# DeltaNet and soft mixture of experts on one core: full 32-column inversions on GpSimd, keys multiplied apart from queries, 24 stores and a re-planned order

## The chip, the cores and the metric

The kernel runs on one core of a Trainium2 chip. A core has a matrix engine (TensorE; PE in the profile, its weight loads PEld) and three others: VectorE (DVE), ScalarE (ACT) and GpSimd (POOL). SyncE (SP) only issues transfers. Each engine takes its own instructions in the order in which they were emitted, and waits at the first one whose input is not there. The metric is the device time of one execution in microseconds, less is better. All data are fp32.

## The reference

Two blocks stand one behind the other. The first is a delta-rule attention over B=4 batches, H=8 heads, S=768 positions and D=48 elements. For every batch and head, with k normalised and a 48x48 state that starts at zero:

```python
for t in range(S):
    y[t]  = q[t] @ state
    v_old = k[t] @ state
    state = state + beta[t] * outer(k[t], v[t] - v_old)
```

Its output, as x of 3072 tokens by 384, goes into a soft mixture of experts with 8 experts of 4 slots each and a hidden size of 1024:

```python
logits = x @ phi                                   # 3072 x 32 slots
d = softmax(logits, over tokens)
c = softmax(logits, over slots)
slot_input = d.T @ x                               # 32 x 384
slot_out[e] = relu(slot_input[e] @ w1[e]) @ w2[e]  # 4 slots an expert
out = c @ slot_out                                 # 3072 x 384
```

w1 and w2 are 25 MB together. The first block is a recurrence over 768 positions, the second needs all tokens before its slots are complete.

## The kernel before

**Chunks and groups.** The sequence is cut into 24 chunks of C=32 positions. A tile of a chunk has 128 partitions: 4 batches times 32 positions. Four chunks make a group, and there are 6 groups (0 to 5). Within a chunk the recurrence is solved as a triangular system: with G the products of the keys with one another, and N the strictly lower part of -beta times G, the rows W that are added to the state are (1 - N)^-1 times beta (V - K state). Since G does not depend on the state, the inverse of a group's 32 matrices a chunk row (4 chunks x 8 heads, each 32x32) can be worked out ahead. Only what needs the state is sequential.

**Ahead of the state**, for every chunk: K and Q are loaded (48 KB a batch and chunk, four transfers each) and transposed on PE (`turn`, L446), ACT copies both to X (L455), and PE multiplies the keys with keys and queries at once (`products`, L473). The key part goes to G (ACT L486, DVE L490), the query part with a triangular mask to AT (DVE L494). In group 0 alone, keys and queries are transposed and multiplied by separate calls, all the keys first. DVE then transposes G to lb (L509), so that one partition holds one 32x32 matrix, and `invert` follows:

- low, on POOL (L513): the two diagonal 16x16 blocks of lb, with mask and sign, into tt.
- the norms of the keys from the diagonal of G (ssq, norm: L518 to L540; two of the steps are on ACT), and gm = beta over the squared norm.
- N, on DVE (L544): the rows times gm. One, on POOL (L547): a diagonal of ones.
- the elimination, `step` (L558 the product, L562 the sum): for columns j = 1 to 14 of both 16x16 blocks, 2 x j x (15-j) elements in each instruction. On DVE for group 0, on POOL for the others.
- tS and tD (L571, L578), the scaled inverse and a spread copy of one block; on the same engine as the elimination. Then DT, the transpose back (L582), and oD, Dn (L584, L587) on DVE.
- the joins: two sets of small PE products (L601, L607) with DVE in between (X16 L615) and after (DT- L623) give the block below the diagonal from the two 16x16 inverses.
- DTb (L632): two copies, masked by the parity of the batch; on ACT (in group 0 one on DVE).

**The chain**, 24 chunks one after another: PE multiplies keys and queries with the state (R, QS: L655), DVE takes R from V (L668), PE multiplies with the inverse (W, L678), DVE and ACT copy W masked into two halves (L689, L694), POOL adds the halves to Wcall (L698), PE adds K^T W to the state's bank (L706), which ACT and DVE copy to St (L716, L720). Off this loop PE multiplies AT with Wcall (AU, L731) into the bank that holds QS, and ACT copies it to Y (L737). V is scaled by the norms on POOL (L638, 24 times).

**Routing**, once a group: Y is transposed (L755), the logits (L768) with a running maximum over tokens, the softmax over slots (Call, on POOL, L814) and the sums over tokens (L827, L833). **Experts** after the last group: L1001 and L1039 the two layers, then the output: 12 times two products (po, L1079) into two banks, a copy of both (ACT L1089, DVE L1086), and four stores of 96 KB (L1096), 48 in all, every second one on SP's queue and the others on ACT's.

**What sets the order.** All of this is emitted through `Plan`, a list scheduler that runs when the program is built. Each operation has an engine, an estimated duration, the keys that it reads and writes, and the PSUM banks that it takes. `order` gives each operation a tail: its duration plus the longest tail behind it. It then steps through a modelled time, and lets each engine take, among the operations that can start first, the one with the longest tail. PE is modelled with the throttle of its clock, and where PE would idle long enough a filler product is put in (L404), which writes to a free bank and is read by nobody. The order that results is the order of every engine's queue. There are six banks for this work, of which four may be held by work ahead of the chain, and two that hold the state. K has 11 buffers, Q 5, V 7, X and AT 9 each, G and DTb 2. A load can start only when its buffer is free. All input loads are issued by SP, but for one in four of the first four K's and every second of V, which ACT issues; beta and phi come by POOL's queue. The weights (L894, SP) go into buffers of the first block as these become free.

Of the kernel before, what the change touches and what calls it, by code (L numbers as in the profile page):

```python
# [10 lines left out]
ALU = mybir.AluOpType  # L11
ACT = mybir.ActivationFunctionType
PSUM = bass.MemoryType.PSUM

# [13 lines left out]
class Plan:  # L28
# [12 lines left out]
    WINDOW, KEEP, DENSE, BONUS, FORCE = 2.5, 0.46, 0.5, 40.0, 0.0  # L41

# [6 lines left out]
    def op(self, eng, us, fn, r=(), w=(), acq=None, rel=None, pre=(), bias=0.0, land=0.0, name="", touch=None):  # L49
# [3 lines left out]
        o.eng, o.us, o.fn, o.acq, o.rel, o.bias, o.land, o.name = eng, us, fn, acq, rel, bias, land, name  # L53
# [50 lines left out]
    def order(self):  # L104
# [3 lines left out]
        clock, held = {}, {"bulk": 0, "chain": 0}  # L108
# [47 lines left out]
        while len(done) < n:  # L156
# [3 lines left out]
            for eng, ls in ready.items():  # L160
                now = clock.get(eng, 0.0)
                cand = []
                for t, o in ls:
                    t = max(t, now)
                    taken = []
                    for a in o.acq:
                        if a.b is None:
                            room = self.room(a, held, taken)
                            if room is None:
                                t = None  # L170
                                break
                            taken += range(room[1], room[1] + a.n)
                            t = max(t, room[0])
                    if t is not None:
                        cand.append((t, o))
                if cand:
                    first = min(c[0] for c in cand)

                    def worth(c):
                        return c[1].tail + (bonus if eng == "PE" and c[1].area > self.DENSE * c[1].us  # L180
                                            else 0.0), -c[1].at
# [25 lines left out]
            if o.eng == "PE":  # L207
                idle = clock.get("PE", 0.0)
                while self.fill and idle >= self.fill[3] and (
# [8 lines left out]
                    f.eng, f.at, f.name, f.start = "PE", -1, "fill", idle  # L218
                    end = array(idle, self.fill[0], self.fill[1], 2)
                    f.us, idle, f.end = end - idle, end, end  # L220
                    t = max(t, idle)
                    done.append(f)
                    n += 1
                us = array(t, us, o.area, o.passes) - t
            o.start, o.end = t, t + us
# [27 lines left out]
def kernel(  # L253
# [60 lines left out]
    tt = buf([P, 2, QC, QC], "tt")  # L314
    pr = buf([P, 2 * 7 * 8], "pr")
    tS = buf([P, C, C], "tS")
    DT = buf([P, U, C], "DT")
    Gl = buf([P, U, QC], "Gl")
    DTb = ring(2, [P, U, 2, C], "DTb")
    tD, oD = buf([P, QC, 2, QC], "tD"), buf([P, U, QC], "oD")  # L320
    gmx = buf([P, 2, QC], "gmx")
    Dn = buf([P, U // 2, C], "Dn")
    X16 = buf([P, U // 2, 2, QC], "X16")
# [43 lines left out]
    for t in Y:  # L367
# [22 lines left out]
    low = buf([P, QC, QC], "low")  # L390
    nc.gpsimd.memset(low, -1.0)
    nc.gpsimd.affine_select(out=low, in_=low, compare_op=ALU.is_ge, fill=0.0, base=-1,
                            pattern=[[1, QC], [-1, QC]], channel_multiplier=0)
    sel = buf([P, NSL], "sel")
    nc.vector.tensor_reduce(sel, ident.rearrange("p (c t) -> p t c", t=NSL), axis=AX.X, op=ALU.add)
    for t in (Kall, Qall):
        nc.vector.memset(t.rearrange("p n (h d) -> p (n h) d", d=DP)[:, :, D:DP], 0.0)
    nc.gpsimd.memset(tS, 0.0)
    nc.gpsimd.memset(Dn, 0.0)
    nc.gpsimd.memset(St, 0.0)  # L400
    nc.vector.memset(bank[:, 6:8, :], 0.0)
# [22 lines left out]
    def load_v(n):  # L424
        load(v, V[n % NV], ("V", n % NV), n, ("SP", "ACT"), [("V", n % NV)])
# [4 lines left out]
    def load_small():  # L430
# [6 lines left out]
        D_(0.32, lambda: nc.vector.tensor_copy(beta_, bt), r=[("bt", p) for p in range(0, P, H)],  # L437
# [10 lines left out]
    def turn(n, which):  # L448
        h = Banks(len(which), "bulk")
        for j, i in enumerate(which):  # L450
            plan.op("PE", turns(4), lambda i=i, j=j: turn_one(n, i, h, j),
                    r=all4("Q", n % NQ) if i else all4("K", n % NK), w=[(h, j)], acq=h,
# [46 lines left out]

    sm = [{a: buf([P, C], f"{a}{i}") for a in ("ssq", "nrm", "rn", "gm", "nT")} for i in range(2)]  # L500

    def invert(m):
        z = m % 2
        ssq, nrm, rn, gm = (sm[z][a] for a in ("ssq", "nrm", "rn", "gm"))
        gr, t = G[z], tt
        fl = lb.rearrange("p t s -> p (t s)")
        gk = [("G", z, c) for c in range(GC)]
        fast = m == 0
        D_(dve(1024, False, 1.75), lambda: nc.vector.transpose(fl, gr.rearrange("p u t -> p t u")),  # L509
           r=gk, w=["lb"], name="lb")  # L510
        for s in range(2):
            b = slice(QC * s, QC * s + QC)
            plan.op("POOL", pool(256, 2.5), lambda s=s, b=b: nc.gpsimd.tensor_tensor(  # L513
                t[:, s], lb[:, b, b], low, op=ALU.mult), r=["lb"], w=["tt"], name="low")
        if fast:
# [16 lines left out]
        D_(0.38, lambda: nc.vector.reciprocal(rn, nrm), **a)  # L532
        D_(0.22, lambda: nc.vector.tensor_tensor(rn, rn, ssq, op=ALU.mult), **a)
        D_(0.22, lambda: nc.vector.tensor_tensor(nrm, nrm, rn, op=ALU.add), **a)
        D_(0.22, lambda: nc.vector.tensor_scalar(nrm, nrm, 0.5, 1e-6, op0=ALU.mult, op1=ALU.add),
           **a)
        D_(0.38, lambda: nc.vector.reciprocal(rn, nrm), **a)
        D_(0.22, lambda: nc.vector.tensor_tensor(gm, rn, rn, op=ALU.mult), r=[("nrm", z)],
           w=[("gm", z)], name="norm")
        D_(0.22, lambda: nc.vector.tensor_tensor(gm, gm, beta_[:, m], op=ALU.mult),  # L540
           r=[("gm", z), "beta"], w=[("gm", z)], name="norm")
        for s in range(2):
            b = slice(QC * s, QC * s + QC)
            D_(dve(256, False, 0.9), lambda s=s, b=b: nc.vector.tensor_tensor(  # L544
                t[:, s], t[:, s], gm[:, b].unsqueeze(2).broadcast_to([P, QC, QC]), op=ALU.mult),
                r=["tt", ("gm", z)], w=["tt"], name="N")
        plan.op("POOL", 0.15, lambda: nc.gpsimd.memset(  # L547
            t.rearrange("p s i k -> p s (i k)")[:, :, 0:QC * QC:QC + 1], 1.0), r=["tt"], w=["tt1"],
            name="one")
        D_(0.2, lambda: nc.vector.transpose(sm[z]["nT"], nrm), r=[("nrm", z)], w=[("nT", z)],  # L550
           name="nT")
        on, eng = ("DVE", nc.vector) if fast else ("POOL", nc.gpsimd)

        def step(j, part):
            w = QC - 1 - j
            o = pr[:, 0:2 * w * j].rearrange("p (s i k) -> p s i k", s=2, i=w)
            if part == 0:
                eng.tensor_tensor(  # L558
                    o, t[:, :, j, 0:j].unsqueeze(2).broadcast_to([P, 2, w, j]),
                    t[:, :, j + 1:QC, j].unsqueeze(3).broadcast_to([P, 2, w, j]), op=ALU.mult)  # L560
            else:
                eng.tensor_tensor(t[:, :, j + 1:QC, 0:j], t[:, :, j + 1:QC, 0:j], o, op=ALU.add)  # L562

        for j in range(1, QC - 1):
            n = 2 * j * (QC - 1 - j)
            for part in range(2):
                plan.op(on, dve(n, False, 0.86) if fast else pool(n, 2.2),
                        lambda j=j, part=part: step(j, part), r=["tt"], w=["tt", "pr"], name="elim")
        for s in range(2):
            b = slice(QC * s, QC * s + QC)  # L570
            plan.op(on, dve(256) if fast else pool(256, 2.5), lambda s=s, b=b: eng.tensor_tensor(  # L571
                tS[:, b, b], t[:, s], gm[:, b].unsqueeze(1).broadcast_to([P, QC, QC]),
                op=ALU.mult), r=["tt", "tt1", ("gm", z)], w=["tS"], name="tS")
        D_(0.2, lambda: nc.vector.tensor_tensor(
            gmx, gm[:, 0:QC].unsqueeze(1).broadcast_to([P, 2, QC]),
            odd.unsqueeze(2).broadcast_to([P, 2, QC]), op=ALU.mult), r=[("gm", z)], w=["gmx"],
           name="tD")
        plan.op(on, dve(512) if fast else pool(512, 2.5), lambda: eng.tensor_tensor(  # L578
            tD, t[:, 0].rearrange("p i s -> p s i").unsqueeze(2).broadcast_to([P, QC, 2, QC]),
            gmx.rearrange("p x s -> p s x").unsqueeze(3).broadcast_to([P, QC, 2, QC]),  # L580
            op=ALU.mult), r=["tt", "tt1", "gmx"], w=["tD"], name="tD")
        D_(dve(1024, False, 1.75), lambda: nc.vector.transpose(  # L582
            DT.rearrange("p u t -> p t u"), tS), r=["tS"], w=["DT"], name="DT")
# [576 lines left out]
```

## Time and profile before

| | |
|---|---|
| time, median of 3 runs | 347.65 us (343.53 to 349.06) |
| profiled execution, its own time | 350.11 us |
| its span (first to last instruction) | 348.3 us |
| granted TensorE clock, mean | 0.931 |
| PE busy | 278.8 us, 80% |
| PE weight loads busy | 222.1 us, 64% |
| DVE busy | 178.4 us, 51% |
| ACT busy | 130.7 us, 38% |
| POOL busy | 132.0 us, 38% |
| Wcall sums on POOL (L698) | 24 of 1002 ns, 24.0 us |
| fillers (L404) | 232 products, 37.9 us |
| input loads of K, Q, V | 48.0 KB each, 2.4 to 2.8 us from issue to landing |

Everything is taken from one profiled execution; the times are of executions without the profiler. A row of the groups view reads: line, engine, operation, output<-input, partitions x elements, how many, then busy time and the mean of one in ns, then the engine's idle time just ahead of them with what ended it. In the chain view the work that ended last is followed back through what released it, so its shares add to the span. In a timeline row stand the start in us from the span's start, how long, the engine, the line and the operation. An engine that is busy little may still set the time, where others wait for it in order; and one that is busy much may be idle in the place that counts.

### The profile page before, as it was taken

The page shows a single profiled execution, that of the slowest core. Times are in us where ns is not written, and L with a number is a line of the kernel's source. Part 1 is how long each engine was busy: PE and PEld are TensorE (multiplying, and loading weights), DVE is VectorE, ACT ScalarE, POOL GpSimd, SP SyncE. Part 2 cuts the span into 40 slices and gives each one's busy share as a digit, 9 for nine tenths or more (in the row PEclk, how much of TensorE's full clock was granted, in tenths as well). Part 3 has the DMA queues.
Part 4 walks back from the last instruction along what each step waited for, and adds up shares of the span by engine and source line. Part 5 has one row for each costly group of instructions (what it writes and reads, how often), then busy time and mean ns, then how long its engine had stood idle before and what let it go on. Part 6 is the DMA issues. An engine that isn't in the chain of part 4 may idle for free.

```text
span 348.3 us, 16203 instructions
## 1 busy us (share of the span) xinstructions
PE 278.8 (80%) x7182; PEld 222.1 (64%) x7182; DVE 178.4 (51%) x384; ACT 130.7 (38%) x258; POOL 132.0 (38%) x263
## 2 busy tenths in 40 slices
PE   2873096997959986898988878998787899999970
PEld 1762096886848776787867667886666787334430
DVE  7098919746561753836576484664642632210600
ACT  1321054543453625564436444453164434011050
POOL 9710401488128740289504891258811110000000
PEclk9987579998998999999899999999999999999955
DMA  6755643154445333324342405475458389697287
GB/s 120 134 85 91 100 67 59 28 88 81 75 106 86 66 55 70 66 49 77 52 80 77 111 10 145 110 193 164 135 173 332 104 272 307 212 389 282 75 259 208
DMA packets 90853, 45.24 MB, mean 130 GB/s; under 512 B 80400, under 2 KB 83600, under 8 KB 90784
## 3 DMA queue, kind: packets, MB, share of 16 engines
q1 hardware_dynamic: 74176, 39.15, 44.0%
q10 hardware_dynamic: 16064, 4.92, 6.5%
q8 instruction: 56, 0.92, 1.1%
q0 software_dynamic: 544, 0.15, 0.3%
q14 instruction: 13, 0.11, 0.1%
HBM read 39.47 MB, written 4.72 MB: 127 GB/s over the span
## 4 chain that ended last, share of the span: by engine, by line
PE 53%; POOL 17%; DVE 13%; issue 9%; DMA 3%; ACT 2%; SPq 0%; POOLq 0%; DVEq 0%; ACTq 0%
PE bank L655 6%; PE bank L731 6%; PE bank L446 5%; PE bank L678 5%; POOL tt L562 4%; PE bank L473 4%; POOL pr L558 4%; PE bank L404 4%; PE bank L1079 4%; PE bank L706 3%; PE bank L1039 3%; PE bank L1001 3%; POOL Wcall L698 3%; PE bank L601 3%; POOL bt L435 2%
## 5 line engine op out<-in xcount | busy, mean ns | idle before, releaser
L698 POOL TENSOR_TENSOR Wcall<-W 128x384 f32<-128x384 f32 x24 | 24.0, 1002 | 63.2 <-ACT W L694 59.1
L655 PE MATMUL bank<-St,X 128*32 128x96 f32 x1472 | 37.5, 248 | 8.6 <-issue 6.1
L455 ACT ACTIVATE X<-bank 128x1024 f32<-128x1024 f32 (+1 forms) x28 | 25.3, 902 | 42.2 <-PE bank L446 35.8
L404 PE MATMUL bank<-ident 128*128 128x128 f32 x232 | 37.9, 307 | 2.5 <-issue 2.5
L655 PEld LDWEIGHTS bank<-St,X 128*32 128x32 f32 x1472 | 31.1, 110 | 13.2 <-issue 8.8
L404 PEld LDWEIGHTS bank<-ident 128*128 128x128 f32 x232 | 32.8, 214 | 6.5 <-issue 4.8
L446 PE MATMUL bank<-ident,Kall 128*128 128x128 f32 x96 | 19.0, 331 | 20.9 <-DVE ATall L494 13.1
L473 PE MATMUL bank<-X 48*64 48x128 f32 (+1 forms) x896 | 28.4, 266 | 7.7 <-ACT X L455 3.4
L731 PE MATMUL bank<-Wcall,ATall 64*64 64x48 f32 x768 | 27.8, 221 | 8.3 <-POOL Wcall L698 6.9
L731 PEld LDWEIGHTS bank<-Wcall,ATall 64*64 64x64 f32 x768 | 24.8, 136 | 11.7 <-POOL Wcall L698 9.6
L694 ACT ACTIVATE W<-bank,par 128x192 f32<-128x192 f32 x48 | 17.6, 418 | 38.8 <-PE bank L678 28.4
L720 DVE TENSOR_TENSOR St<-bank,half 128x768 f32<-128x768 f32 x23 | 21.9, 952 | 19.3 <-PE bank L706 19.1
L473 PEld LDWEIGHTS bank<-X 48*64 48x64 f32 x896 | 23.3, 139 | 10.4 <-issue 5.1
L678 PE MATMUL bank<-R,DTb 64*64 64x48 f32 x736 | 26.3, 220 | 2.5 <-issue 1.4
L513 POOL TENSOR_TENSOR tt<-lb,low 128x256 f32<-128x256 f32 x12 | 8.5, 734 | 52.0 <-DVE lb L509 52.0
L446 PEld LDWEIGHTS bank<-ident,Kall 128*128 128x128 f32 x96 | 13.0, 168 | 24.0 <-DVE ATall L494 13.4
L678 PEld LDWEIGHTS bank<-R,DTb 64*64 64x64 f32 x736 | 23.6, 135 | 6.1 <-issue 3.6
L716 ACT ACTIVATE St<-bank 48x384 f32<-48x384 f32 x46 | 22.3, 484 | 13.3 <-PE bank L706 12.4
L562 POOL TENSOR_TENSOR tt<-tt,pr 128x28 f32<-128x28 f32 (+6 forms) x70 | 24.4, 348 | 5.5
L490 DVE SCALAR_TENSOR_TENSOR G<-bank,par,G 128x128 f32<-128x128 f32 x48 | 15.0, 344 | 20.8 <-ACT G L486 20.8
L558 POOL TENSOR_TENSOR pr<-tt 128x28 f32<-128x28 f32 (+6 forms) x70 | 23.7, 338 | 4.9
L689 DVE TENSOR_TENSOR W<-bank,par 128x384 f32<-128x384 f32 x24 | 13.3, 555 | 23.6 <-PE bank L678 23.4
(211 smaller groups left out, 533.6 us busy)
## 6 DMA issues: line engine op xcount, KB each, us to landing
Qall<-in_q_dram SPq DMA_DIRECT2D x96, 48.0 KB, 2.5
Kall<-in_k_dram SPq DMA_DIRECT2D x92, 48.0 KB, 2.4
X<-in_moe_w_dram SPq DMA_DIRECT2D x7, 512.0 KB, 4.2
X<-in_moe_w_dram SPq DMA_DIRECT2D x7, 384.0 KB, 6.4
Vall<-in_v_dram ACTq DMA_DIRECT2D x48, 48.0 KB, 2.7
Vall<-in_v_dram SPq DMA_DIRECT2D x48, 48.0 KB, 2.8
Kall<-in_moe_w_dram SPq DMA_DIRECT2D x4, 512.0 KB, 4.1
ATall<-in_moe_w_dram SPq DMA_DIRECT2D x3, 512.0 KB, 3.6
```

Of the source, the lines that this page charges most:

```text
L404: plan.fill = (0.223, 0.213, 0.1, 6.0, lambda b: nc.tensor.matmul(bank[:, b, 0:P], lhsT=ident, rhs=ident, start=True, stop=True, skip_grou ...
L446: nc.tensor.transpose(at(h, j)[:, P * e:P * e + P], src[:, P * e:P * e + P], ident)
L455: plan.op("ACT", act(512 * len(which)), lambda: nc.scalar.activation(dst, at(h, 0, 2) if len(which) > 1 else at(h).unsqueeze(1), ACT.Copy) ...
L473: nc.tensor.matmul(at(h, g)[rb, 2 * w * C * e:2 * w * C * (e + 1)], lhsT=x[r, 0, e, rb], rhs=x[r, which[0]:which[0] + w, e, rb], start=(e ...
L558: eng.tensor_tensor(o, t[:, :, j, 0:j].unsqueeze(2).broadcast_to([P, 2, w, j]), t[:, :, j + 1:QC, j].unsqueeze(3).broadcast_to([P, 2, w, j ...
L562: eng.tensor_tensor(t[:, :, j + 1:QC, 0:j], t[:, :, j + 1:QC, 0:j], o, op=ALU.add)
L655: nc.tensor.matmul(at(h)[rb, 2 * D * e:2 * D * e + 2 * D], lhsT=x[:, i, e, rb], rhs=St[:, b, e].rearrange("p g d -> p (g d)"), start=(e == ...
L678: nc.tensor.matmul(at(hw, u // HQ)[rb, D * (u % HQ):D * (u % HQ) + D], lhsT=t[rb, H * c + u].rearrange("p j t -> p (j t)"), rhs=rhs[rb, u, ...
L698: plan.op("POOL", pool(384), lambda: nc.gpsimd.tensor_tensor(wc, ww[:, :, 0, :], ww[:, :, 1, :], op=ALU.add), r=wk, w=[("Wc", n % 2)], nam ...
L716: plan.op("ACT", act(384), lambda r=r, g=g: nc.scalar.activation(St[r].rearrange("p (i j) e g d -> p i g (j e) d", i=2)[:, 0, g], bank[r, ...
L720: D_(dve(768, True), lambda: nc.vector.tensor_tensor(St.rearrange("p (i j) e g d -> p i (j e) g d", i=2)[:, 1], bank[:, SB + 1, 0:H * D].r ...
L731: nc.tensor.matmul(at(hy)[rb, D * u:D * u + D], lhsT=a[rb, u % 2, u // 2, :], rhs=wc[rb, u, :], start=(n == 0 and u == 0), stop=True, skip ...
```

## The change

1. Groups 1 to 5: tt is a full 32x32 matrix in a ring of two. The elimination runs over columns 1 to 30 of it, j x (31-j) elements an instruction, all on POOL. `low` becomes gl, a mask times gm, on DVE (1024 elements); N and tS are one DVE instruction of 1024 elements each; tD, Dn, X16, T16 and DT- are gone from these groups.
2. Group 0: `invert_joined` holds the 16-column elimination with joins, with its elimination, tS and tD on DVE as before and `low` there too. Its buffers are laid over DTb[1] and yT.
3. The norm has one DVE step fewer: beta is kept four times as large, and Y is scaled by 0.5 in its copy.
4. Wcall is no longer a sum on POOL but one ACT copy of both W banks.
5. In groups 0 to 2 (`APART`), keys are transposed and multiplied ahead of and apart from the queries; before, in group 0 alone. All V loads are issued by SP.
6. Each output tile has two stores of 192 KB instead of four of 96 KB, one on SP's queue and one on ACT's.
7. `Plan`: a table of biases by engine and name that are added to the tails, a modelled cost for a change of PE's tile shape, a window of 0.3 us on PE within which the longest tail is taken, begin times for each engine, and a bias of 3.0 on R. The memsets of pads, St and the state's banks are planned too. The fillers fall from 116 calls to 85 (two products each).

```diff
+BIAS = {
+    "ACT.DTb": -2.5, "ACT.G": 15.1, "ACT.Gl": -26.1, "ACT.S": -28.5, "ACT.W": 0.9, "ACT.Wc":
...
+    BEGIN = {"SP": 0.85, "ACT": 0.9, "POOL": 2.3, "DVE": 3.0, "PE": 2.0}
+
+    TILES = {"W": "64", "AU": "64", "S": "64", "prod": "64", "R": "state", "QS": "state", "turn": "turn",
...
+    DRAIN = {"64": 0.15, "state": 0.17, "turn": 0.093, "32": 0.113, "fill": 0.2}
+    SAME = {"64": 0.045, "state": 0.055}
...
+        o.bias = bias + BIAS.get(f"{eng}.{name}", 0.0)
...
+        def change(o):
+
+            if last is None:
+                return 0.0
+            a, b = self.TILES.get(last), self.TILES.get(o.name)
+            return self.SAME.get(a, 0.0) if a == b and a else self.DRAIN.get(a, 0.35)
...
+                        if eng == "PE":
+                            t = max(t, now + change(o))
                         cand.append((t, o))
                 if cand:
-                    first = min(c[0] for c in cand)
+                    first = min(c[0] for c in cand) + (0.3 if eng == "PE" else 0.0)
...
-        load(v, V[n % NV], ("V", n % NV), n, ("SP", "ACT"), [("V", n % NV)])
+        load(v, V[n % NV], ("V", n % NV), n, ("SP",), [("V", n % NV)])
...
+        D_(dve(1024), lambda: nc.vector.tensor_tensor(
+            gl[z], low, gm.unsqueeze(1).broadcast_to([P, C, C]), op=ALU.mult),
+            r=[("gm", z)], w=[("gl", z)], name="low")
...
+        if fast:
+            invert_joined(z, gr, gm, gk)
+        else:
+            D_(dve(1024), lambda: nc.vector.scalar_tensor_tensor(
+                t, lb, -1.0, gm.unsqueeze(2).broadcast_to([P, C, C]), op0=ALU.mult, op1=ALU.mult),
+                r=["lb", ("gm", z)], w=[("tt", z)], name="N")
...
+            def step(j, part):
+                w = C - 1 - j
+                o = pr[on][:, 0:w * j].rearrange("p (i k) -> p i k", i=w)
+                if part == 0:
+                    eng.tensor_tensor(
+                        o, t[:, j, 0:j].unsqueeze(1).broadcast_to([P, w, j]),
+                        t[:, j + 1:C, j].unsqueeze(2).broadcast_to([P, w, j]), op=ALU.mult)
+                else:
+                    eng.tensor_tensor(t[:, j + 1:C, 0:j], t[:, j + 1:C, 0:j], o, op=ALU.add)
+
+            for j in range(1, C - 1):
...
+            D_(dve(1024), lambda: nc.vector.tensor_tensor(
+                t, t, gl[z], op=ALU.mult), r=[("tt", z), ("tt1", z), ("gl", z)], w=[("tt", z)],
+               name="tS")
...
-        plan.op("POOL", pool(384), lambda: nc.gpsimd.tensor_tensor(
-            wc, ww[:, :, 0, :], ww[:, :, 1, :], op=ALU.add), r=wk, w=[("Wc", n % 2)], name="Wc")
+        plan.op("ACT", act(384), lambda: nc.scalar.activation(
+            wc.rearrange("p (i u) d -> p i (u d)", i=2), at(hw, 0, 2)[:, :, 0:HQ * D], ACT.Copy),
+            r=[hw], w=[("Wc", n % 2)], rel=hw, name="Wc")
...
-                for b in range(B):
-                    dst = out[b * S:(b + 1) * S].rearrange("(n t) f -> t n f", t=C)[
-                        :, GC * m + 2 * s:GC * m + 2 * s + 2, :]
...
+                for i in range(2):
+                    dst = out.rearrange("(b n t) f -> n b t f", b=B, t=C)[GC * m + 2 * s + i]
+                    plan.op("SP" if i else "ACT", 0.5, lambda i=i, o=o, dst=dst: (
+                        nc.sync if i else nc.scalar).dma_start(
+                            out=dst, in_=ob[o][0][:, i]),
+                        r=[("ob", o)], w=[("out", m, s, i)], land=0.55, name="store")
...
+        apart = m < APART
         for n in ns:
             load_k(n)
-            if m:
+            if not apart:
                 load_q(n)
...
+        if apart:
+            for n in ns:
+                turn(n, (0,))
+                products(n, (0,))
+            for n in ns:
+                load_q(n)
         for n in ns:
             load_v(n)
...
-                turn(n, (0, 1))
-                products(n, (0, 1))
-            else:
-                turn(n, (0,))
-                products(n, (0,))
         invert(m)
         for n in ns:
-            if m == 0:
+            if apart:
                 turn(n, (1,))
                 products(n, (1,))
             scale_v(n)
```

Which engine issues an operation is unchanged but for those named; the order in every queue is not.

## The prediction

> **What bounds the kernel now.** I read the page's busy shares first, then the chain that ended last, the waits, and the groups of instructions with shapes kept apart. The chain by engine:
>
> ```profile
> PE 53%; POOL 17%; DVE 13%; issue 9%; DMA 3%; ACT 2%; SPq 0%; POOLq 0%; DVEq 0%; ACTq 0%
> ```
>
> POOL is busy 38% of the span but ends the chain for 17%, so it matters in places. The list of waits shows where: the AU product (L731) waits for the POOL sum Wcall (L698), which stands behind the elimination in POOL's queue.
>
> ```profile
> PEld bank L731 <- POOL Wcall L698: 9.6, 14, 2.3
> ...
> PE bank L731 <- POOL Wcall L698: 6.9, 9, 2.1
> ```
>
> The chain in order of time shows the same: POOL holds it from 65.8 to 80.2, 148.1 to 163.4, 197.5 to 203.9 and 230 to 244. The first W product of each group (L678) starts, by the timeline, at 62.5, 110.1, 146.1, 190.2, 230.3 and 264.7 us; the last AU ends at 289.1, and 59.2 us of experts and stores follow. The last four steps, which produce nothing for a later group, take 24.4 us, so a step alone needs 6.1.
>
> **What POOL gets.** The change takes 24 Wcall sums (24.0 us) and, per group, the 16-column elimination and tS, tD, low off POOL, and gives it a 32-column one: 30 columns, two instructions each, j(31-j) elements. That is 60 instructions and 2 x 4960 = 9920 elements, where there were 28 and 2240. Price, from groups by form:
>
> ```profile
> L638 POOL TENSOR_TENSOR Vall<-Vall,nT 128x384 f32<-128x384 f32 x24 | 20.5, 875 | 9.8 <-DVE pr L558 7.4 <-DMA Vall<-in_v_dram 2.3
> ...
> L578 POOL TENSOR_TENSOR tD<-tt,gmx 128x512 f32<-128x512 f32 x5 | 6.9, 1381 | 0.0
> L562 POOL TENSOR_TENSOR tt<-tt,pr 128x112 f32<-128x112 f32 x10 | 4.1, 414 | 0.8
> ...
> L558 POOL TENSOR_TENSOR pr<-tt 128x112 f32<-128x112 f32 x10 | 4.0, 399 | 0.8
> ...
> L562 POOL TENSOR_TENSOR tt<-tt,pr 128x28 f32<-128x28 f32 x10 | 2.5, 250 | 0.8
> L558 POOL TENSOR_TENSOR pr<-tt 128x28 f32<-128x28 f32 x10 | 2.4, 244 | 0.4
> ```
>
> From 28 to 112 elements an instruction grows by 0.16 us, 1.9 ns an element over a base of 0.194; 10.4 us of idle before the page's 140 such instructions add 0.074. So 60 x 0.268 = 16.1 us fixed. The elements are dearer or cheaper by shape: (829 median - 194)/384 = 1.65 ns on L638, whose second operand is broadcast along the row as in the product step; 2.32 on L578. No row has 240 elements, so the bounds are 16.1 + 9920 x 1.65 or 2.32 ns = 32.5 and 39.1 us. I take 1.65 for the product and 1.95 (L562's own) for the sum: 16.1 + 8.2 + 9.7 = **34.0 us** a group, against 11.8 now (65.94 to 77.78).
>
> [...]
>
> **The schedule this gives.** POOL's order in the changed program is known from its build: the five eliminations run one behind another, with the V scalings (0.85 each) among them. I walk it by rows.
>
> *Start.* Group 0's inversion stays on DVE. Its DT transpose ended at 39.7. Added ahead of it are gl (1024 elements: 0.42 for 256 on L544, 0.556 for 384 on L518, so 1.06 ns an element, 1.24 us) and tD (0.95); gone are a norm step, and the waits for POOL that stretched L533, L534 and one L562 (about 1.5). So about 40. Behind it DVE has nT 0.2, G 1.4, lb 2.0, oD 1.0, Dn 0.7, three AT 2.0, X16 0.7, ssq and norm 1.8, N 1.24: group 1's elimination starts at 51.2 instead of 65.9. This is what multiplying keys apart from queries moves: G of group 1 is there by 40, not 56.
>
> *Per group* I add 34.0, 0.85 for each V inside (3, 3, 1, 1, 3), and the turn-around before the next. Groups 2 and 5 have N ready before: two or one V, tS 1.24, memset: 3.1 and 2.25. For groups 3 and 4 the built DVE order puts the norm and N behind the previous group's tS and DT: V 0.85 + tS 1.24 + DT 2.0 + norm and R 2.1 + N 1.24 + 0.15 = 7.6. Starts and ends: 51.2-87.8, 90.9-127.4, 135.0-169.9, 177.5-212.3, 214.6-251.1. Then tS, DT, two DTb copies on ACT (2.19), a Call and hops: 6.1. Group 5's first W at 257.2.
>
> *A lock.* DVE instructions with two SBUF inputs and POOL instructions hold each other up:
>
> ```profile
> 225.82 1.00 POOL L698 TENSOR_TENSOR Wcall<-W 128x384 f32<-128x384 f32 x1
> 225.88 0.99 DVE L533 TENSOR_TENSOR rn<-rn,ssq 128x32 f32<-128x32 f32 x1
> ...
> 36.40 1.40 DVE L571 TENSOR_TENSOR tS<-tt,gm 128x256 f32<-128x256 f32 x2
> 36.46 2.02 POOL L638 TENSOR_TENSOR Vall<-Vall,nT 128x384 f32<-128x384 f32 x2 [0.21 <-DMA Vall<-in_v_dram]
> ```
>
> L533 needs 0.19 us alone and took 0.99 behind Wcall; two V scalings, 1.68 alone, took 2.02 beside 0.84 us of tS. Seven long DVE instructions now fall inside eliminations (DTb and gl of group 0/1, N and gl of 2, gl of 3 and 4, N of 5). Each costs POOL between nothing and its 1.24 us, 0 to 8.7 in all. The nearest row gives 0.34 for 0.84; a longer one hides a smaller part in POOL's gaps, so 0.7 each, 4.9. [...] W of group 5 at **262.1**, 2.6 earlier than now.
>
> *Does the chain keep up?* It must do four steps in the 33 us between two inversions. Group 1's took 35.9 (110.1 to 146.0), with 3.1 us of joins (four L601/L607 rows of 0.74 to 0.84) that go. It just does, and then waits; so what the change saves on PE (joins 16.3 us, fills 116 to 85, the order by tiles) is idle there and costs or gives nothing. The keys apart add 8 products (0.69 each half against 1.03: 2.8 us in all) and 8 X copies, in the same cover; with POOL free of charge they would be late.
>
> *Moves.* Wcall on ACT: 24 x 0.49 (L737's size), behind the two W copies; it ends 0.49 us after them, while the S product needs 0.88 before ACT's S copies can start: hidden, and if not, 0.5 a step. AU no longer waits: 0.5 in the last steps. The 48 V loads leave ACT for SP, which then issues 284 input loads at about 0.46 us, 131 us of its queue; K and Q loads and the weights stand behind them. Cover: SP waited 61.6 us for V loads alone and weights came in from 195 on. If the cover goes, a late load shows 2.5 us each. DVE's tS wait holds later G and AT work behind it, for which PE has slack.
>
> *Stores.* In the timeline's end the copies are done at 338.4, yet stores are issued until 345.9:
>
> ```profile
> 337.56 0.81 ACT L1089 ACTIVATE X<-bank 128x768 f32<-128x768 f32 x1 [0.47 <-PE bank L1079]
> ...
> 345.02 0.92 ACTq L1096 DMA_DIRECT2D out_dram<-DTb  x2
> ```
>
> 24 per queue at 0.43 us become 12 of twice the bytes. Then the last copy is followed by one issue and a landing of 2.7 to 4: 342 to 345 instead of 348. I take -4.5.
>
> **Sum.** -2.6 (W of group 5) -0.5 (AU) -4.5 (stores) = -7.6: a span of 340.7, a profiled execution of 342.5 (350.11 now), and 347.65 - 7.6 = **340.0** against the median, since the profiled execution lies 2.5 above it.
>
> **Rivals.**
> - *Cheap elimination*: 1.65 ns throughout and no lock: 340 - 7.5 - 4.9 = 327.6. For it: L638. Against: L562's own rows. 0.20.
> - *Full lock*: 8.7 and 35 us a group: 340 + 3.8 + 5 = 349, no change. For it: L533's row. 0.20.
> - *Slower*: the longer rows cost what L578 cost, 39.1 us: 340 + 25.5 = 365. It decides from 36.9 us a group (2.1 ns an element), where 354.6 is passed; Wcall's row gives 2.1, but strided. 0.14.
> - *POOL does not pace it after all* (the change doesn't act as read): PE's own rate, 53 + 5 x 32.8 + 24 + 54.7 = 296. Everything in POOL's order speaks against. 0.03.
> - Forecast, 333 to 347: 0.43.
>
> Two per cent is about what a measurement of this kernel tells from no change. About half of the forecast's case lies under 340.7: faster 0.22 + 0.20 + 0.03 = 0.45, same 0.41, slower 0.14. Range 324 to 356: it leaves out most of the slower case and the ends of the cheap ones, under 0.2.
>
> **What would show it.** Eliminations of about 34 us, one right behind another, POOL over 60% busy; in the chain POOL's share up and L731's waits for POOL gone; PE waiting for DTb at each group's first W; first W of group 1 near 94 and of group 5 near 262; the last store within 5 us of the last copy. Wrong if an elimination instruction of 240 elements is far from 0.62 us, or if first W's come without a wait for DTb.

## The result and the profile after

The changed kernel takes **371.65 us** (median of 4 runs, 370.27 to 372.32) against 348.36 (median of 4 runs) before: a ratio of 1.075 with an interval of 1.062 to 1.087. I had forecast 340.0, range 324 to 356. It is slower, and outside the range. Executions of one program fall into a faster and a slower state, and the ratios here and below compare those in the faster one. The profiled execution has a span of 370.6 us.

The chain that ended last, by engine and by line, from the page of the changed kernel:

```profile
POOL 39%; PE 22%; DMA 10%; DVE 10%; issue 7%; SPq 4%; ACT 1%; ACTq 1%; POOLq 0%; DVEq 0%
POOL prPOOL L605 17%; POOL tt L609 17%; DMA out_dram<-tt 4%; SPq L457 4%; DMA out_dram<-Y 4%; PE bank L1092 3%; PE bank L1130 3%; POOL bt L478 2%; PE bank L742 2%; PE bank L517 2%; PE bank L447 2%; PE bank L765 2%; POOL Vall L724 2%; PE bank L489 2%; PE bank L794 2%
```

POOL's share went from 17% to 39%, of which 34% stand in the two elimination lines, as forecast. But DMA has 10%, and it names the output. The row of the DMA engines' busy share, in tenths for 40 slices of the span, first before, then after:

```profile
DMA  6755643154445333324342405475458389697287
```
```profile
DMA  5655444444454553463025635383769694122222
```

Before, the last six slices are 6 to 9 tenths busy, but for one 2, in which the output copies start. After, the last six (56 us) stand at 1 to 2 tenths. That is where the time went, as the stretches show:

| stretch, us | forecast | before | after |
|---|---|---|---|
| start of the first POOL elimination | 51.2 | 65.9 | 49.4 |
| end of the last | 251.1, with the lock 256.0 | | 256.8 |
| first W of group 5 | 262.1 | 264.7 | 262.4 |
| from there to the first output product (po) | 60.2 | 60.7 | 54.3 |
| from there to the end of the span | 18.4 | 22.9 | 53.8 |

At the first W of group 5 the walk is right to within half a microsecond, but only because its errors cancel: the first elimination starts 1.8 us earlier than forecast, the five take 189.0 us in place of 184.2 (with the lock), and the gaps between them 18.3 in place of 20.6. Runs with the same order up to there have this W between 260.3 and 262.4, so half a microsecond is also less than they differ by. The rest failed twice, once in my favour (5.9 us) and once against me (35.4 us). The end of the changed kernel, in the chain in order of time (start, duration, what):

```profile
320.98 14.54 DMA out_dram<-tt
335.89 13.09 DMA out_dram<-Y
349.06 2.65 ACTq L1186
351.81 0.81 ACT X L1180
```

In this chain 14.5 and 13.1 us lie between the issue of a 192 KB store and the step that had waited for it (the landings themselves are not in this trace). ACT's first output copy stands behind stores in ACT's queue and waits for them, until 328.0. The copies are done at 352.6, where 338.4 of before less the forecast 3.1 would be 335.3, and the stores run to 370.

### The profile page after: what moved, and what is told of

The parts are those of the page before. It is cut to its first block, busy times and chain, and to the rows that moved or that the text cites. A ratio compares the mean times of both kernels' runs of the same rounds, so it can differ in the third digit from the quotient of the medians.

```text
span 370.6 us, 14088 instructions
## 1 busy us (share of the span) xinstructions
PE 265.6 (72%) x6096; PEld 212.1 (57%) x6096; DVE 180.0 (49%) x360; ACT 137.3 (37%) x285; POOL 200.1 (54%) x372
## 3 DMA queue, kind: packets, MB, share of 16 engines
HBM read 39.47 MB, written 4.72 MB: 119 GB/s over the span
## 4 chain that ended last, share of the span: by engine, by line
POOL 39%; PE 22%; DMA 10%; DVE 10%; issue 7%; SPq 4%; ACT 1%; ACTq 1%; POOLq 0%; DVEq 0%
POOL prPOOL L605 17%; POOL tt L609 17%; DMA out_dram<-tt 4%; SPq L457 4%; DMA out_dram<-Y 4%; PE bank L1092 3%; PE bank L1130 3%; POOL bt L478 2%; PE bank L742 2%; PE bank L517 2%; PE bank L447 2%; PE bank L765 2%; POOL Vall L724 2%; PE bank L489 2%; PE bank L794 2%
## 5 line engine op out<-in xcount | busy, mean ns | idle before, releaser
L609 POOL TENSOR_TENSOR tt<-tt,prPOOL 128x30 f32<-128x30 f32 (+9 forms) x150 | 79.8, 532 | 11.4
L605 POOL TENSOR_TENSOR prPOOL<-tt 128x30 f32<-128x30 f32 (+9 forms) x150 | 78.8, 525 | 10.8
L499 ACT ACTIVATE X<-bank 128x512 f32<-128x512 f32 (+1 forms) x36 | 26.3, 741 | 49.4 <-PE bank L489 49.2
L517 PE MATMUL bank<-X 48*64 48x64 f32 (+1 forms) x1152 | 35.4, 270 | 9.7 <-DVE ATall L538 6.3
L724 POOL TENSOR_TENSOR Vall<-Vall,nT 128x384 f32<-128x384 f32 x24 | 23.6, 991 | 12.6 <-DMA Qall<-in_q_dram 12.3
L447 PE MATMUL bank<-ident 128*128 128x128 f32 x170 | 28.9, 322 | 0.0
L819 PE MATMUL bank<-Wcall,ATall 64*64 64x48 f32 x768 | 27.7, 222 | 1.6 <-issue 1.6
L819 PEld LDWEIGHTS bank<-Wcall,ATall 64*64 64x64 f32 x768 | 26.0, 139 | 2.5 <-issue 1.8
L804 ACT ACTIVATE St<-bank 48x384 f32<-48x384 f32 x46 | 22.3, 485 | 7.7 <-PE bank L794 6.8
L628 ACT ACTIVATE DTb<-DT,par 128x1024 f32<-128x1024 f32 x11 | 12.1, 1141 | 34.9 <-DVE DT L620 34.9
L617 DVE TENSOR_TENSOR tt<-tt,gl 128x1024 f32<-128x1024 f32 x5 | 8.7, 1746 | 33.2 <-POOL tt L609 33.2
L794 PE MATMUL bank<-W,Kall 64*48 64x96 f32 x736 | 22.6, 265 | 1.5 <-DVE W L776 1.5
L1170 PE MATMUL bank<-so,cT 32*128 32x384 f32 x48 | 13.1, 667 | 13.6 <-ACT X L1180 6.9
```

The lines of the kernel that those rows point to most:

```text
L447: plan.fill = (0.223, 0.213, 0.1, 6.0, lambda b: nc.tensor.matmul(bank[:, b, 0:P], lhsT=ident, rhs=ident, start=True, stop=True, skip_grou ...
L499: plan.op("ACT", act(512 * len(which)), lambda: nc.scalar.activation(dst, at(h, 0, 2) if len(which) > 1 else at(h).unsqueeze(1), ACT.Copy) ...
L517: nc.tensor.matmul(at(h, g)[rb, 2 * w * C * e:2 * w * C * (e + 1)], lhsT=x[r, 0, e, rb], rhs=x[r, which[0]:which[0] + w, e, rb], start=(e ...
L605: eng.tensor_tensor(o, t[:, j, 0:j].unsqueeze(1).broadcast_to([P, w, j]), t[:, j + 1:C, j].unsqueeze(2).broadcast_to([P, w, j]), op=ALU.mult)
L609: eng.tensor_tensor(t[:, j + 1:C, 0:j], t[:, j + 1:C, 0:j], o, op=ALU.add)
L724: plan.op("POOL", pool(384), lambda: nc.gpsimd.tensor_tensor(V[n % NV], V[n % NV], sm[m % 2]["nT"][:, H * c:H * c + H].unsqueeze(2).broadc ...
```

## Experiments

Where nothing else is said, an experiment starts from the changed kernel. Times are medians, ratios are against runs of the kernel before on the same chip. The medians of the kernel before lie between 349.7 and 352.0 in these sets, so a difference of 2 us between two experiments tells nothing by itself.

### The stores: their shape, their size, or their order

Three theories. *Shape*: a store is spread over as many DMA engines as it has entries in its outermost dimension. *Size*: 192 KB is slow as such. *Order*: ACT's copies stand behind its stores.

**The 48 stores of before, put back** (after_48):

```diff
-                for i in range(2):
-                    dst = out.rearrange("(b n t) f -> n b t f", b=B, t=C)[GC * m + 2 * s + i]
+                for b in range(B):
+                    dst = out[b * S:(b + 1) * S].rearrange("(n t) f -> t n f", t=C)[
+                        :, GC * m + 2 * s:GC * m + 2 * s + 2, :]
...
```

> The changed kernel with the 48 stores of 96 KB of the kernel before (32 rows outermost), all else and every queue's order as changed. Shape theory (a store is spread over as many DMA engines as it has entries in its outermost dimension: 4 batches in the changed store, 32 rows before): the output products start at 317 as in the changed kernel, and 22.9 us follow as in the kernel before, a span of 340 and a time near 341. Size theory (a store of 192 KB is slow as such): the same 341. Order theory (the biases put ACT's copies behind its store issues, and that costs the time): 360 to 372, since the order stays.

Measured: **341.54 us** (340.06 to 342.20), ratio 0.975 (0.970 to 0.981), span 339.8. The stores alone turn a kernel 2.5% faster than before into one 7.5% slower. Order as the main cause falls: the queues stand as they did, and 30 us are gone.

**24 stores with rows outermost** (after_24t): as many as in the change and as large, each of one batch and four chunks.

```diff
+        four = lambda x: x[:, 0:4 * Dm].rearrange("p (c d) -> p c d", c=4)
+        obw = [Y[0][:, :, 0:Dm], Y[1][:, :, 0:Dm], four(yT.rearrange("p k c t -> p (k c t)")),
...
-                            out=dst, in_=ob[o][0][:, i]),
...
+                        dst = out[b * S:(b + 1) * S].rearrange("(n t) f -> t n f", t=C)[
+                            :, GC * m:GC * m + GC, :]
...
+                                out=dst, in_=obw[m][C * b:C * b + C]),
...
```

> The changed kernel with 24 stores of 192 KB, 12 a queue, but each of one batch and four chunks, so that 32 rows are outermost and not 4 batches; the copies go to wider buffers. Shape theory: near 338 to 342, the DMA share in the end 0.6 to 0.75 instead of 0.25. Size theory: 365 to 372, as changed. Order theory: 360 to 372.

Measured: 343.32 us (342.74 to 344.85), ratio 0.983 (0.976 to 0.989). Size falls: the same bytes in the same number of stores, and 28 us less. The time is 1.3 above what was expected by shape. A store here needs two copies, so the first is issued 6.5 us behind the first output product (after_48: 2.0). From there to the end it is 20.2 us (after_48: 21.9; the kernel before: 20.9), and in the windows from 322 to 335 the DMA engines move 241 to 287 GB/s.

**48 stores of two batches** (after_48b): small, but with 2 outermost.

```diff
+                    for x in range(2):
+                        dst = out.rearrange("(b n t) f -> n b t f", b=B, t=C)[
+                            GC * m + 2 * s + i, 2 * x:2 * x + 2]
...
```

> The changed kernel with 48 stores of 96 KB, each of two batches of one chunk, so that only 2 are outermost. Shape theory: 2 of 16 DMA engines at work in a store, a DMA share of 0.125 in the end, 4.72 MB at some 46 GB/s are 100 us behind 319: a time near 420 (less where the two queues' stores fall on different engines). Size theory: 341. Order theory: 360 to 372.

Measured: 417.65 us (one run), near the 420 of the shape theory and of no other. **The new stores in the kernel before** (before_24):

> The kernel before with the changed kernel's 24 stores alone, the order of all else as before. Shape theory and size theory: output products from 325 as before, then 51 us of stores: a span near 378, a time of 372 to 380. Order theory: 343 to 350, no change or a little less. My forecast's own step (12 issues fewer a queue): 343.

Measured: 379.68 us (376.81 to 383.79), ratio 1.082 (1.073 to 1.092), where my forecast's own step had 343. The windows of the end show why (columns: stretch, its length, busy time of PE, PEld, DVE, ACT and POOL with the number of instructions, the granted clock, the DMA engines' busy share, GB/s). The changed kernel, 4 outermost:

```profile
330.00:345.00 15.00, 3.81 (x10) 1.00 (x8) 0.00 (x0) 2.43 (x3) 0.00 (x0) 0.50 0.27 100
345.00:369.00 24.00, 0.00 (x0) 0.00 (x0) 0.00 (x0) 1.62 (x2) 0.00 (x0) 0.50 0.27 100
```

48 stores of two batches, 2 outermost:

```profile
320.00:360.00 40.00, 3.94 (x16) 1.10 (x12) 1.32 (x2) 0.81 (x1) 0.00 (x0) 0.56 0.13 49
```

The kernel before with the new stores, 4 outermost:

```profile
350.00:379.00 29.00, 0.00 (x0) 0.00 (x0) 0.00 (x0) 0.00 (x0) 0.00 (x0) 0.50 0.26 97
```

24 stores with 32 rows outermost:

```profile
326.00:330.00 4.00, 1.35 (x4) 0.20 (x2) 0.00 (x0) 0.81 (x1) 0.00 (x0) 0.50 0.96 273
330.00:335.00 5.00, 0.00 (x0) 0.00 (x0) 0.00 (x0) 1.62 (x2) 0.00 (x0) 0.50 0.94 287
```

A share of 0.26 to 0.27 of 16 engines is 4.2 to 4.3 of them, 0.13 is 2.1; the rate is 97 to 100 and 49 GB/s, some 25 GB/s for each entry of the outermost dimension where there are 2 or 4. With 32 rows nearly all engines work (0.94 to 0.96). (2, 4 and 32 entries are what was measured.) In the changed kernel two queues have several stores in flight, and still only four engines' worth of time is used. (The profile gives the share, not which engines; that both queues' stores fall on the same ones is my reading of the sum and was not shown.) 4.72 MB at 97 to 100 GB/s are 47 to 49 us, nearly all of the 51.8 between the first store's issue at 318.8 and the end of the span.

### Does POOL set the pace?

**Half of each elimination left out** (half_elim, with the 48 stores):

```diff
             def step(j, part):
+                if j > 15:
+                    return
```

> The changed kernel with 48 stores, and of each elimination on GpSimd only columns 1 to 15: columns 16 to 30 (30 of 60 instructions) are left out, so the inverses are incomplete; the order of all else stays. POOL theory (eliminations one behind another set the pace of the groups): each is 17 us shorter, POOL falls under what a group takes on PE (33 us), and the first W of group 5 comes 40 to 50 us earlier, a time of 290 to 305. Rival (PE or the chain sets the pace, and POOL is only busy): 330 to 342.

Measured: 314.21 us (one run), 27 us under after_48 and between the two expectations. The first W of group 5 starts at 234.4, 27.8 us earlier and not 40 to 50. The pace theory holds in direction and not in size: the five eliminations fall from 189.1 us to 101.4, the gaps between them grow from 18.3 to 69.1, and 27 came back. In the chain of this run POOL has 4% (after_48: 43%):

```profile
PE 57%; DVE 14%; ACT 7%; DMA 6%; SPq 4%; issue 4%; POOL 4%; ACTq 1%; DVEq 0%; POOLq 0%
```
```profile
POOL tt L597 <- DVE tt L594: 27.3, 5, 8.4
```

The second line (waits: total, times, longest) says that POOL now waits for N from DVE at each start; its V scalings wait another 19.2 us for loads of V. Other work is the next bound, 27 us below, at least in this order; that it is PE is suggested by its 57% of the chain and was not tested.

**Wcall back on POOL** (wc_pool, with the 48 stores; the diff is the one shown above, reversed):

> The changed kernel with 48 stores and the Wcall sum back on POOL. POOL theory: 16 to 20 sums of 0.9 to 1.0 us fall between the first elimination and the last, so 355 to 362. Rival (POOL has room for them in the waits between the eliminations): 341 to 345.

Measured: 364.14 us (361.35 to 365.17), 22.6 above after_48 and 2.1 above what the POOL theory gave. The eliminations from start to end, measured in each run's trace, show that most of it is POOL's time and not gaps of a new order: together they grow from 189.1 to 211.3 us, with 19 of the 24 sums and two Calls inside them, and the gaps between them shrink from 18.3 to 15.0. The last one ends 18.9 us later; the other 3.7 come behind it.

**Two eliminations on DVE** (lend24, with the 48 stores):

```diff
-    LEND = ()
+    LEND = (2, 4)
```

> The changed kernel with 48 stores and the eliminations of groups 2 and 4 on DVE (the same instructions on the other engine). POOL theory: POOL has three eliminations of 36 us in place of five and no longer sets the pace; DVE gets 2 x 20 us more, the chain's own DVE steps wait behind single instructions of 0.3 us: 305 to 325. Rival (DVE instructions with two SBUF inputs hold POOL's up and the reverse, and the chain's steps on DVE wait): 335 to 350.

Measured: 381.91 us (381.45 to 384.98), ratio 1.089 (1.082 to 1.096). My theory missed by 57 us, measured from the upper end of what it gave, and the rival by 32. DVE did group 2's elimination in 24.9 us (102.6 to 127.5), faster than POOL's 36.9. But in the new plan group 3's N came at 149.4, 22 us behind it on the same queue, and POOL had no elimination between group 1's end at 85.0 and group 3's start at 150.7. In those 22 us DVE stood twice for copies of G by ACT, the last of which let it go on at 141.1; lb and the norm came behind that. Five eliminations that were to overlap became a row again. POOL's work alone does not make the time; when each elimination's inputs come through DVE's queue counts as well.

### The order

**No biases** (no_bias, with the 48 stores): the table `BIAS` is empty.

> The changed kernel with 48 stores and an empty table of biases, so that the order comes from the planner's tails alone; the costs for changes of tiles stay. POOL theory: the eliminations still follow one another, first W of group 5 within 5 us of 262, a time of 338 to 348. Rival (the order carries the gain): 350 to 360.

Measured: 362.84 us (362.47 to 363.17), ratio 1.032 (1.027 to 1.037), 21.3 above after_48. The rival was right in direction; the time is 2.8 above its range. **V scaled on DVE** (scale_dve, with the 48 stores):

```diff
-        plan.op("POOL", pool(384), lambda: nc.gpsimd.tensor_tensor(
+        plan.op("DVE", dve(384), lambda: nc.vector.tensor_tensor(
             V[n % NV], V[n % NV],
```

> The changed kernel with 48 stores and the 24 scalings of V on DVE in place of POOL. POOL theory: some 15 scalings of 0.83 us leave the time between the first elimination and the last, 12 us, and DVE holds POOL up a little more: 328 to 337. Rival (the planned order decides how far apart the eliminations stand, and a new plan with biases made for another one leaves gaps, as the run without biases did): 345 to 365.

Measured: 367.79 us (367.37 to 369.63), 26 above. The rival again, and again 2.8 above its range. Where POOL waits for N (L594; L577 without biases) in the three kernels, first the changed one, then no_bias, then scale_dve:

```profile
POOL tt L597 <- DVE tt L594: 14.9, 3, 9.7
```
```profile
POOL tt L580 <- DVE tt L577: 41.1, 5, 15.3
```
```profile
POOL tt L597 <- DVE tt L594: 59.5, 4, 22.5
```

From the traces, us:

| kernel | first elimination starts | five eliminations | four gaps | last one ends |
|---|---|---|---|---|
| after_48 | 48.1 | 189.1 | 18.3 | 255.5 |
| wc_pool | 48.1 | 211.3 | 15.0 | 274.4 |
| no_bias | 41.0 | 178.8 | 54.6 | 274.4 |
| scale_dve | 47.9 | 185.5 | 47.1 | 280.4 |

Both without biases and with V on DVE POOL itself is faster; the gaps eat it. The table of biases is worth 36 us of gaps; against that, with it the first elimination starts 7 us later and the five take 10 us more, so the last one ends 19 us earlier. The waits name N: in the order that it gives, DVE has N ready nearer to the time at which POOL wants it. It also means that a part of this change can't be undone alone: a new estimate anywhere gives a new order.

**Wcall on ACT alone, in the kernel before** (before_wc):

> The kernel before with Wcall copied by ACT from the W banks, and nothing else of the change. If POOL's place in the chain (17%) was the sums that stood behind the elimination: L731's waits for POOL go and the time falls to 335 to 343. Rival (only the eliminations themselves held the chain, and the sums were waited for beside it): 345 to 350.

Measured: ratio 1.017 (1.011 to 1.023, from three executions), longer by less than two per cent, the profiled execution 354.39 us. Both theories missed. Its chain by engine and by line:

```profile
PE 48%; DVE 14%; DMA 11%; POOL 11%; issue 8%; SPq 2%; ACT 2%; ACTq 0%; POOLq 0%; DVEq 0%
PE bank L655 6%; POOL tt L562 5%; POOL pr L558 5%; DMA Kall<-in_k_dram 4%; PE bank L446 4%; PE bank L473 4%; PE bank L678 4%; PE bank L1080 3%; PE bank L732 3%; DMA Vall<-in_v_dram 3%; PE bank L707 3%; PE bank L1040 3%; PE bank L404 3%; PE bank L1002 3%; DVE DT L582 3%
```

POOL fell from 17% to 11%, and DMA rose from 3% to 11%, of which late loads of K and V are 7%. The new plan has loads that come later than they are wanted. Whether the move itself would pay in the old order was not tried by itself, so that AU's waits for POOL held the kernel before is not shown.

### The end

**ACT's copies ahead of its stores** (tail_t2, with the 48 stores):

```diff
-    "ACT.hr": 3.2, "ACT.lT": 10.6, "ACT.loadK": -10.3, "ACT.norm": -3.8, "ACT.ob": -70.0,
-    "ACT.store": 53.7, "ACT.yT": 19.1, "DVE.AT": -14.6, "DVE.DT": 1.3, "DVE.DT-": -19.9,
+    "ACT.hr": 3.2, "ACT.lT": 10.6, "ACT.loadK": -10.3, "ACT.norm": -3.8, "ACT.ob": 33.8,
+    "ACT.store": 0.0, "ACT.yT": 19.1, "DVE.AT": -14.6, "DVE.DT": 1.3, "DVE.DT-": -19.9,
```

> The changed kernel with 48 stores and, in the end alone, ACT's six output copies ahead of its stores instead of behind the twelve stores of DVE's copies (two biases changed; nothing else moves). If ACT's 12.0 us of waiting in front of its first copy set the end: 333 to 337. If the bytes of the stores set it (4.72 MB, 200 to 280 GB/s in the windows of the end): 339 to 342, no change.

Measured: **338.23 us** (337.92 to 339.70), ratio 0.965 (0.958 to 0.971), 3.3 under after_48 and the fastest kernel of this study that leaves nothing out. The first ACT copy in after_48, and in this kernel (start, duration, what, the wait ahead of it):

```profile
326.12 0.81 ACT L1180 ACTIVATE Y<-bank 128x768 f32<-128x768 f32 x1 [11.99 <-DMA out_dram<-X]
```
```profile
315.09 0.81 ACT L1180 ACTIVATE Y<-bank 128x768 f32<-128x768 f32 x1 [2.76 <-PE bank L1170]
```

The copies no longer wait 12 us, and all are done at 325.0 in place of 335.9. Little of that shows in the time, which lies between the two expectations. Of the 3.6 us between the two profiled spans, 1.8 stand ahead of the first output product (at 315.9 and at 314.1), where nothing was changed; from there to the end it is 22.1 us in place of 23.9. In both kernels the DMA engines then move the stores' bytes: in after_48 4.72 MB in the 21.9 us from the first store's issue at 317.9 to the end, 216 GB/s in the mean (a share of 0.78 to 0.92 in the windows from 322 to 335), and here in the 20.3 us from 315.9, 233 GB/s. So the order of ACT's queue costs some 2 us at the end. They are not a part of the 30 us, which after_48 won with ACT's copies still behind its stores.

## Why the prediction was wrong, and where it was right

**Price of the elimination: right.** Forecast 34.0 us a group. Groups by form, the changed kernel:

```profile
L609 POOL TENSOR_TENSOR tt<-tt,prPOOL 128x240 f32<-128x240 f32 x10 | 6.8, 676 | 0.8
L605 POOL TENSOR_TENSOR prPOOL<-tt 128x240 f32<-128x240 f32 x10 | 6.2, 616 | 0.8
```

The forecast was 0.62 for such an instruction. A line through the medians of all forms from 30 to 240 elements gives 0.184 us + 1.83 ns an element for the product and 0.191 + 1.99 for the sum (taken: 1.65 and 1.95). All medians of a group sum to 30.2 us; with 59 gaps of 0.074 that is 34.6, and 3 us more than forecast over the five groups.

**The lock: undersized.** Taken 4.9 us with bounds of 0 and 8.7. The timeline of the changed kernel:

```profile
80.18 1.49 DVE L594 SCALAR_TENSOR_TENSOR tt<-lb,gm 128x1024 f32<-128x1024 f32 x1
80.67 1.41 POOL L609 TENSOR_TENSOR tt<-tt,prPOOL 128x184 f32<-128x184 f32 x1
81.72 1.43 DVE L586 TENSOR_TENSOR gl<-low,gm 128x1024 f32<-128x1024 f32 x1
82.15 1.34 POOL L605 TENSOR_TENSOR prPOOL<-tt 128x168 f32<-128x168 f32 x1
83.58 0.54 POOL L609 TENSOR_TENSOR tt<-tt,prPOOL 128x168 f32<-128x168 f32 x1
```

Beside the DVE instruction a POOL instruction of 0.6 or less takes 1.4. Nine of the 300 are longer than their form's median by more than 0.25 us, eight of them by 0.83 to 0.96; in all 7.4 us over the five groups. That is nearer to my upper bound, seven times DVE's whole 1.24 us, than to the row that I went by, 0.34 us lost beside 0.84 of tS. I read the rest, to DVE's 1.2 us, as the part that falls into POOL's own gap or instruction; that was not measured.

**The gaps: right.** Forecast 3.1, 7.6, 7.6, 2.3; measured 2.5, 7.0, 8.0, 0.8. I took them from the order as built, where groups 3 and 4 have their N behind the previous group's tS and DT. The run without biases shows how much hung on that order, which the diff alone would not have told.

**"Idle there and costs or gives nothing": wrong, by 5.9 us.** I kept the stretch from group 5's first W to the output at 60.7 less 0.5. The windows of this stretch, up to the last AU and behind it (the first busy column is PE), before:

```profile
264.70:289.10 24.40, 22.13 (x610) 18.77 (x610) 9.47 (x20) 9.60 (x24) 4.41 (x5) 1.00 0.70 219
289.10:325.40 36.30, 35.61 (x335) 17.03 (x335) 7.68 (x23) 6.34 (x14) 0.40 (x1) 1.00 0.75 276
```

and after:

```profile
262.50:282.70 20.20, 19.07 (x569) 16.26 (x570) 9.05 (x20) 10.07 (x28) 0.80 (x2) 1.00 0.72 224
282.70:316.80 34.10, 32.14 (x319) 15.17 (x319) 7.78 (x23) 6.34 (x14) 0.40 (x1) 1.00 0.70 253
```

PE is idle for 3 us in both and has 57.7 us of work before and 51.2 after. The transposes of Y in this stretch fall from 20 to 12 and the filler products from 56 to 30: routing was done earlier, ahead of group 5's first W, and what was planned to fill gaps was not needed. Without the table of biases (no_bias) the stretch up to the first output product is 56.5 us, so most of this gain is not the table's. PE time saved under a cover is not lost if work behind the cover can move into it.

**The stores: the step that failed.** I had "24 per queue at 0.43 us become 12 of twice the bytes", -4.5 us. Two errors. First, issue did not bound the end: 24 stores with rows outermost gave 343.32, not less than the 341.54 of 48, and from the first store's issue to the end they took 20.2 us, where the 48 of the kernel before took 20.9. In that kernel's end the DMA engines were nearly full:

```profile
330.00:335.00 5.00, 5.00 (x20) 2.25 (x20) 1.66 (x2) 2.32 (x3) 0.00 (x0) 0.62 0.91 279
335.00:340.00 5.00, 2.52 (x8) 0.77 (x6) 0.00 (x0) 2.43 (x3) 0.00 (x0) 0.50 0.88 241
```

I read the issue rows as a cause without reading the DMA row of the same slices. Second, the new store's outermost dimension is 4 where it was 32, and I gave this no cost at all. No row of before shows a large transfer with so few entries outermost, so it should have been bounded like the other unknowns. Measured: 53.8 us in the place of 22.9, +30.9.

**Sum.** -8.6 up to the output (forecast -3.1) and +30.9 behind it (forecast -4.5) are +22.3, from 348.3 to 370.6. My slower rival named 365 for dearer eliminations; the side came out and the mechanism did not. Without its stores the prediction would have been 344.5, and after_48 took 341.54, but that this is near is luck in part: its span is 8.5 us under before, made of 2.5 at the first W of group 5, 7.0 from there to the output and 1.0 lost behind it, where I had 3.1 in all. What bears out the walk of the inversions are the starts and ends in the traces, not this time.

**What was to show it.** Eliminations run one behind another. L819, the AU product, no longer waits for POOL. The first W of group 1 starts at 96.3 (near 94). PE sits idle for DTb only once, for 8.9 us. By my own words that speaks against me; but POOL's 39% of the chain and half_elim speak for the pace, and elsewhere the plan put other work and fillers into the wait, so this sign was a poor one. POOL is busy 54% of the span and not over 60%; without the long stores, in after_48, it is 59%. The last store is issued 2.6 us behind the last copy, and the span runs on for another 15.

## What to carry to other kernels

Look at the outermost dimension of a transfer before its size and number: in these runs it set how many DMA engines worked (a share of 0.13 with 2 entries, 0.26 to 0.27 with 4, up to 0.96 with 32), and a coalescing that puts four batches in front of the rows cost more than everything else gained. Before crediting fewer issues, read the DMA engines' busy share in the same slices; at 0.9, half as many issues won nothing here. In a planned kernel a part can't be judged by undoing it alone, so compare what each run's trace shows (lengths of the pacing steps, and the gaps between them), not only the times.

## What the runs showed of the hardware

- Stores from two queues with 4 outermost entries kept 0.26 to 0.27 of the 16 DMA engines busy (97 to 100 GB/s), with 2 entries 0.13 (49 GB/s), with 32 rows, in after_24t, 0.93 to 0.96 (241 to 287 GB/s).
- On DVE the elimination's instruction of 240 elements took 0.41 us alone (lend24), on POOL 0.62 to 0.68 (the changed kernel); a whole elimination, with what else stood inside it, 24.9 and 36.9 us.
- In the changed kernel eight elimination instructions on POOL (L605, L609) beside N, gl or tS on DVE (1024 elements, both inputs in SBUF; 1.2 us alone) lost 0.83 to 0.96 us each. The 18 that lay inside a transpose of 1024 elements on DVE (L557, L620: one input, 1.9 to 2.0 us) took their form's median within 0.02 us.
